# Retention plus two FFN layers on one Trainium2 core: the full-array state products of a chunk moved ahead of its half-width products

## The chip, the cores and the metric

One core of one Trainium2 chip runs the kernel. The metric is device time in microseconds (us) of one execution; kernels are compared by the median of several runs. The engines are named as in the profile: PE (matmuls) with PEld (its weight loads, which have rows of their own), ACT, DVE, POOL, and SP, which issues the DMAs.

## What is computed

Three stages in a row. The first is a retention layer over 2 batches, 8 heads, 768 tokens, head width 64; the other two are feed-forward layers of width 512 to 2048 to 512, the first with Mish, the second with ELU. Cut to its core:

```python
gamma = 1.0 - 2.0 ** (-5.0 - np.arange(H))          # one decay per head
for t in range(S):
    state = gamma * state + k[:, :, t] (outer) v[:, :, t]
    y[:, :, t] = scale * q[:, :, t] @ state
x = y as (B*S, H*D)                                  # 1536 x 512
h = x @ w_in;  x = (h * tanh(softplus(h))) @ w_out   # layer 0
h = x @ w_in2; out = elu(h) @ w_out2                 # layer 1
```

## The kernel before

**Retention.** The recurrence is cut into 12 chunks of 128 tokens, two batches by six positions; chunk `c` belongs to batch `c % 2` and is number `i = c // 2` in its batch. Heads go in four pairs `j`, with `r` = 0, 1 for the head inside a pair. `scores(c)` multiplies keys by queries (16 weight loads, 64 rows each, line 201), and DVE multiplies the result by the decay mask into `at` (line 211). `scale_chunk(c)` lets POOL make `kd` (keys with decay, line 173) and `qd` (queries with decay, line 188). `attend(c)` then builds the output `y`, a 128 x 512 tile of one PSUM bank: for each pair `j` one full-array product of `state[:, j]` with `qd[:, j]` (line 226, 128 rows by 128 columns; left out for `i = 0`), and on top of it two half-width products of `v` with `at` (line 228, 128 rows by 64 columns, one for each half of the partitions). Eight more half-width products make the chunk's own contribution `st` to the state (line 237, left out for the last chunk of each batch). All four kinds are in plain float32, and the trace shows two records ("passes") for each such product.

After the products, `rest()` evacuates: ACT copies `y` to `xh` (line 246), DVE writes the remainder `xl` (line 247) and adds `st` to `state` (line 252, or copies it, line 257, for `i = 0`).

**FFN.** Each FFN layer runs 48 tiles `n`: `up(n)` is 12 full-array matmuls into `h` (line 276, in the order high weights by high x, low weights by high x, high weights by low x), `mish(n)` on ACT and POOL makes `gh` and `gl` (lines 297 to 299), and `down(n - 3)` is 12 full-array matmuls into four accumulators (line 335). Weights arrive packed: SP fetches a half tile (line 101), ACT takes it apart (lines 108, 110), DVE joins it (lines 119, 125), ACT and POOL split it into a high and a low part `w0h`, `w0l` (for `up`) or `w1h`, `w1l` (for `down`) (lines 138, 139). The staging pool has four buffers, so a fetch waits until DVE has joined an earlier half. The first eight tiles of a group each need a new weight tile; the two blocks of eight tiles behind them use the same weights again.

**Order.** Everything stands in one hand-written order, and each engine runs its own instructions in that order. Chunks 0 to 3 come first. Chunks 4 to 11 are laid between the FFN tiles: `scores(4)` behind `up(0)`, `attend(4)` behind `up(1)`, and so on up to `attend(11)` behind `up(15)`. On ACT and DVE the evacuation of a chunk stands in line with the decoding of weights.

Of the kernel before, what the change touches and what calls it, by code (L numbers as in the profile page):

```python
# [21 lines left out]
NPAIR = H // 2  # L22
# [18 lines left out]
def retention_then_two_ffn(  # L41
# [7 lines left out]
    nc = tc.nc  # L49
# [141 lines left out]
    def psum(tag, name):  # L191
        return (psh if tag == "h" else psa).tile([P, NPAIR, P], F32, tag=tag, name=name)
# [23 lines left out]
    def attend(c, tags=("h", "h")):  # L216

        kv = raw.pop(c)[1]
        at, (qd, kd) = scored.pop(c), scaled.pop(c)
        i = c // B  # L220
        v = kv[:, 1]
        state = states[c % B]
        y = psum(tags[0], "y")
        for j in range(NPAIR):
            if i:
                nc.tensor.matmul(y[:, j], state[:, j], qd[:, j], start=True, stop=False)  # L226
            for r in range(2):
                nc.tensor.matmul(  # L228
                    y[r * D:(r + 1) * D, j], v[:, 2 * j + r], at[:, r, j],
                    start=not i, stop=True,  # L230
                )
        if i < CPB - 1:
            st = psum(tags[1], "st")
            for j in range(NPAIR):
                for r in range(2):
                    sl = slice(r * D, (r + 1) * D)
                    nc.tensor.matmul(  # L237
                        st[sl, j, sl], kd[:, 2 * j + r], v[:, 2 * j + r], start=True, stop=True
                    )

        def rest():
            b, o = divmod(c, CPT)
            if o == 0:
                x[b] = new_x(b)
            xh, xl = (a[:, :, o * P:(o + 1) * P] for a in x[b])
            nc.scalar.copy(out=xh, in_=y)  # L246
            nc.vector.tensor_tensor(out=xl, in0=y, in1=xh.bitcast(F32), op=ALU.subtract)
            if i < CPB - 1:
                for r in range(2):
                    sl = slice(r * D, (r + 1) * D)  # L250
                    if i:
                        nc.vector.tensor_tensor(
                            out=state[sl, :, sl], in0=st[sl, :, sl], in1=state[sl, :, sl],
                            op=ALU.add,
                        )
                    else:
                        nc.vector.tensor_copy(state[sl, :, sl], st[sl, :, sl])

        return rest

    def new_x(b):
        return tuple(
            xpool.tile([P, KT, TB], F32R, tag=f"x{n}{b}", name=f"x{n}{b}") for n in "hl"
        )
# [100 lines left out]
    with tc.manual_schedule():  # L365
# [54 lines left out]
        scores(1, th)()  # L420
        scale_chunk(2)
        attend(0, tb)()
        scores(2, ta)()
        load_chunk(4)
        scale_chunk(3)
        scores(3, th)()
        join()
        attend(1, th)()
        split_w()
        attend(2, tb)()  # L430
        join()
        attend(3, ta)()
# [116 lines left out]
```

## Time and profile before

| | us |
|---|---|
| median of 3 runs | 594.63 |
| lowest, highest | 593.89, 594.97 |
| the profiled execution's own time | 593.98 |
| its span (first to last instruction) | 592.2 |
| PE busy in the span | 581.0 |
| PEld busy | 472.2 |
| DVE, ACT, POOL busy | 290.7, 275.1, 270.5 |
| granted TensorE clock | full speed throughout (1.0) |

A busy time is the union of an engine's records. The records of matmuls overlap one another, so that a busy PE may still be losing time between them: for PE one reads the distances of the starts beside the busy time.

### The profile page before, as it was taken

What the parts mean: (1) busy time and instruction counts of PE and PEld (TensorE: products, weight loads), DVE (VectorE), ACT (ScalarE), POOL (GpSimd) and SP (SyncE); (2) the same over time, 40 slices, a digit from 0 to 9 for tenths busy, and PEclk for the clock granted to TensorE, in tenths of its full rate; (3) what the DMA queues carried; (4) which work ended last, traced back from release to release, by engine and by line L of the source; (5) the groups of instructions that cost most, each with busy time, mean ns of one, the idle gap of its engine ahead of it and who ended that gap; (6) DMA issues with size and microseconds to landing.
All of it is one profiled execution on the core that took longest, in us unless ns stands there. A gap on an engine that the chain in (4) does not pass through costs nothing.

```text
span 592.2 us, 7565 instructions
## 1 busy us (share of the span) xinstructions
PE 581.0 (98%) x2934; PEld 472.2 (80%) x2934; DVE 290.7 (49%) x354; ACT 275.1 (46%) x482; POOL 270.5 (46%) x200
## 2 busy tenths in 40 slices
PE   6999999999999999999999999999999999999997
PEld 4677777777888888888888888888888888888885
DVE  3787852113234343100483897433797783434534
ACT  1566532312654654222566485533865853333231
POOL 1688764221454554452395487222366552221221
PEclk9999999999999999999999999999999999999999
DMA  8775543200332332000152133000332100100101
GB/s 320 304 249 209 199 162 113 67 0 12 131 107 76 103 106 97 11 1 0 37 177 80 64 107 106 1 1 1 107 107 86 57 1 0 73 0 2 71 2 71
DMA packets 14724, 50.59 MB, mean 85 GB/s; under 512 B 1632, under 2 KB 1632, under 8 KB 14688
## 3 DMA queue, kind: packets, MB, share of 16 engines
q1 hardware_dynamic: 14688, 50.10, 24.3%
q8 instruction: 23, 0.38, 0.2%
q14 instruction: 13, 0.11, 0.1%
HBM read 46.95 MB, written 3.15 MB: 85 GB/s over the span
## 4 chain that ended last, share of the span: by engine, by line
PE 89%; POOL 4%; DMA 3%; DVE 1%; issue 1%; ACT 0%; SPq 0%; POOLq 0%; DVEq 0%; ACTq 0%
PE a L335 43%; PE h L276 42%; DMA xl<-qkv 2%; PE y L228 1%; PE y L226 1%; POOL w0l L139 1%; DMA kv<-qkv 1%; PE sc L201 1%; POOL gl L299 1%; POOL kd L173 1%; POOL qd L188 1%; DMA st<-w 1%; POOL tab L181 0%; DVE acc L348 0%; PE st L237 0%
## 5 line engine op out<-in xcount | busy, mean ns | idle before, releaser
L299 POOL TENSOR_TENSOR gl<-m,gh 128x512 fp32r<-128x512 f32 x48 | 64.2, 1338 | 137.0 <-ACT m L298 117.0
L289 POOL TENSOR_TENSOR gl<-m,gh 128x512 fp32r<-128x512 f32 x48 | 69.5, 1448 | 106.1 <-ACT gh L288 106.1
L119 DVE SCALAR_TENSOR_TENSOR st<-st 128x512 int32<-128x512 int32 x64 | 72.4, 1139 | 90.2 <-ACT st L110 90.0
L276 PE MATMUL h<-xh,w0l 128*128 128x512 f32 x384 | 102.8, 389 | 1.4 <-POOL w0l L139 1.4
L276 PE MATMUL h<-xh,w0h 128*128 128x512 f32 x384 | 103.1, 390 | 0.2 <-ACT xh L246 0.2
L276 PE MATMUL h<-xl,w0h 128*128 128x512 f32 x384 | 102.7, 389 | 0.0
L297 ACT ACTIVATE gh<-h 128x512 fp32r<-128x512 f32 x48 | 28.6, 597 | 135.1 <-PE h L276 135.0
L307 ACT ACTIVATE e<-c 128x512 f32<-128x512 f32 x48 | 30.4, 632 | 123.4 <-DVE c L306 123.3
L276 PEld LDWEIGHTS h<-xh,w0l 128*128 128x128 f32 x384 | 72.0, 188 | 16.7 <-POOL w0l L139 1.8
L306 DVE TENSOR_SCALAR c<-h 128x512 f32<-128x512 f32 x48 | 33.1, 690 | 106.3 <-PE h L276 106.3
L276 PEld LDWEIGHTS h<-xl,w0h 128*128 128x128 f32 x384 | 72.1, 188 | 15.0
L276 PEld LDWEIGHTS h<-xh,w0h 128*128 128x128 f32 x384 | 71.8, 188 | 15.4 <-ACT xh L246 0.4
L125 DVE SCALAR_TENSOR_TENSOR f<-f,st 128x512 int32<-128x512 int32 x64 | 74.6, 1175 | 3.7
L335 PE MATMUL a<-gh,w1h 128*128 128x512 f32 x192 | 76.2, 397 | 0.0
L335 PE MATMUL a<-gh,w1l 128*128 128x512 f32 x192 | 74.8, 390 | 0.0
L335 PE MATMUL a<-gl,w1h 128*128 128x512 f32 x192 | 74.8, 390 | 0.0
L335 PE MATMUL a<-w1h,gh 128*128 128x512 f32 x192 | 74.7, 389 | 0.0
L335 PE MATMUL a<-w1l,gh 128*128 128x512 f32 x192 | 74.7, 389 | 0.0
L335 PE MATMUL a<-w1h,gl 128*128 128x512 f32 x192 | 74.7, 389 | 0.0
L139 POOL TENSOR_TENSOR w0l<-f,w0h 128x512 fp32r<-128x512 f32 x32 | 43.6, 1365 | 32.4 <-ACT w0h L138 27.8
L139 POOL TENSOR_TENSOR w1l<-f,w1h 128x512 fp32r<-128x512 f32 x32 | 45.7, 1427 | 23.3 <-ACT w1h L138 12.3
L108 ACT ACTIVATE f<-st 128x512 f32<-128x512 f32 x64 | 43.0, 672 | 12.8 <-DMA st<-w 7.5
(65 smaller groups left out, 691.9 us busy)
## 6 DMA issues: line engine op xcount, KB each, us to landing
st<-w SPq DMA_DIRECT2D x64, 512.0 KB, 3.6
qk<-qkv SPq DMA_DIRECT2D x10, 512.0 KB, 5.2
kv<-qkv SPq DMA_DIRECT2D x10, 512.0 KB, 5.9
out<-acc SPq DMA_DIRECT2D x12, 256.0 KB, 2.1
xh<-qkv SPq DMA_DIRECT2D x2, 512.0 KB, 9.5
xl<-qkv SPq DMA_DIRECT2D x2, 512.0 KB, 9.7
ct<-consts SPq DMA_DIRECT2D x1, 512.0 KB, 5.4
ct<-consts SPq DMA_DIRECT2D x1, 284.0 KB, 7.2
```

What stands on the lines that cost most here:

```text
L108: nc.scalar.activation(out=f, in_=t[:, :, 1].bitcast(F32), func=AF.Copy, scale=2.0 ** -112)
L119: nc.vector.scalar_tensor_tensor(out=t[:, :, 1], in0=t[:, :, 1], scalar=-(2 ** 31), in1=t[:, :, 0], op0=ALU.bitwise_and, op1=ALU.bitwise_or,)
L125: nc.vector.scalar_tensor_tensor(out=f, in0=f, scalar=3, in1=t[:, :, 1], op0=ALU.logical_shift_left, op1=ALU.bitwise_or,)
L139: nc.gpsimd.tensor_tensor(out=lo, in0=f, in1=hi.bitcast(F32), op=ALU.subtract)
L173: nc.gpsimd.tensor_tensor(out=kd, in0=kv[:, 0], in1=tk[:, i].to_broadcast([P, H, D]), op=ALU.mult)
L276: nc.tensor.matmul(h, u[:, k * P:(k + 1) * P], v[:, k], start=i == 0, stop=i == len(passes) - 1)
L289: nc.gpsimd.tensor_tensor(out=gl, in0=g, in1=gh.bitcast(F32), op=ALU.subtract)
L297: nc.scalar.activation(out=gh, in_=h, func=AF.Mish)
L299: nc.gpsimd.tensor_tensor(out=gl, in0=g, in1=gh.bitcast(F32), op=ALU.subtract)
L306: nc.vector.tensor_scalar(out=c, in0=h, scalar1=0.0, scalar2=None, op0=ALU.min)
L307: nc.scalar.activation(out=e, in_=c, func=AF.Exp)
L335: nc.tensor.matmul(a, l, r, start=first and i == 0, stop=last and i == 2)
```

## The change

In `attend`, the loop over the pairs is split in two. First the four state products of the chunk run one behind the other; then the eight half-width products. Before, each pair's state product stood ahead of its two half-width products, and each state product had `start=True`, which begins a new sum; now only the first of them has it (one clearing of the bank for the whole chunk), and the other three carry no start flag. Chunks with `i = 0` have no state products, and their eight half-width products keep their flags. `skip_group_check=True` only tells the builder not to check the grouping of the sums.

```diff
         y = psum(tags[0], "y")
+        if i:
+            for j in range(NPAIR):
+                nc.tensor.matmul(
+                    y[:, j], state[:, j], qd[:, j],
+                    start=j == 0, stop=False, skip_group_check=True,
+                )
         for j in range(NPAIR):
-            if i:
-                nc.tensor.matmul(y[:, j], state[:, j], qd[:, j], start=True, stop=False)
             for r in range(2):
                 nc.tensor.matmul(
                     y[r * D:(r + 1) * D, j], v[:, 2 * j + r], at[:, r, j],
-                    start=not i, stop=True,
+                    start=not i, stop=True, skip_group_check=True,
                 )
```

What stands on PE for chunk 6, between `up(5)` and `down(2)`, before (`state_98` is the state of batch 0; a row is a run of equal products, the last number its count; in brackets, whose semaphores it waits for):

```order
L276 MATMUL h<-xl_188,w0h 128x512 x4
L226 MATMUL y<-qd,state_98 128x128
L228 MATMUL y<-at,kv 64x128 [waits DMAHW7_49,DVE_49]
L228 MATMUL y<-at,kv 64x128 [waits DVE_49]
L226 MATMUL y<-qd,state_98 128x128
L228 MATMUL y<-at,kv 64x128 x2
L226 MATMUL y<-qd,state_98 128x128
L228 MATMUL y<-at,kv 64x128 x2
L226 MATMUL y<-qd,state_98 128x128
L228 MATMUL y<-at,kv 64x128 x2
L237 MATMUL st<-kv,kd 64x64 [waits PE_49]
```

and at the same place after:

```order
L282 MATMUL h<-xl_188,w0h 128x512 x4
L228 MATMUL y<-qd,state_98 128x128 x4
L234 MATMUL y<-at,kv 64x128 [waits DMAHW7_49,DVE_49]
L234 MATMUL y<-at,kv 64x128 [waits DVE_49]
L234 MATMUL y<-at,kv 64x128 x6
L243 MATMUL st<-kv,kd 64x64 [waits PE_49]
```

The products and the waits are the same; three state products have moved ahead of the first half-width product. (Lines from 226 on have new numbers.)

Chunk 3, the last one ahead of `up(0)`, on PE, before (`state_99` is the state of batch 1, `xl_224` and `xl_117` hold this chunk's `at` and `v`):

```order
L226 MATMUL y<-qd,state_99 128x128 [waits DVE_49,PE_49,Pool_49]
L228 MATMUL y<-xl_224,xl_117 64x128 [waits DMAHW2_49]
L228 MATMUL y<-xl_224,xl_117 64x128
L226 MATMUL y<-qd,state_99 128x128
L228 MATMUL y<-xl_224,xl_117 64x128 x2
L226 MATMUL y<-qd,state_99 128x128
L228 MATMUL y<-xl_224,xl_117 64x128 x2
L226 MATMUL y<-qd,state_99 128x128
L228 MATMUL y<-xl_224,xl_117 64x128 x2
L237 MATMUL st<-xl_117,kd 64x64 [waits PE_49]
L237 MATMUL st<-xl_117,kd 64x64 x7
L276 MATMUL h<-xh_187,w0h 128x512 [waits Activation_49]
```

and after:

```order
L228 MATMUL y<-qd,state_99 128x128 [waits DVE_49,PE_49,Pool_49]
L228 MATMUL y<-qd,state_99 128x128 x3
L234 MATMUL y<-xl_224,xl_117 64x128 [waits DMAHW2_49]
L234 MATMUL y<-xl_224,xl_117 64x128 x7
L243 MATMUL st<-xl_117,kd 64x64 [waits PE_49]
L243 MATMUL st<-xl_117,kd 64x64 x7
L282 MATMUL h<-xh_187,w0h 128x512 [waits Activation_49]
```

Here too only the three later state products have moved; the chunk's first product still waits for DVE and POOL, and `up(0)` for ACT. No other engine's order changes.

## Rows read from the trace of the kernel before

**Rows 1.** The page: busy time by engine (part 1), chain that ended last (part 4).

```profile
PE 581.0 (98%) x2934; PEld 472.2 (80%) x2934; DVE 290.7 (49%) x354; ACT 275.1 (46%) x482; POOL 270.5 (46%) x200
...
PE 89%; POOL 4%; DMA 3%; DVE 1%; issue 1%; ACT 0%; SPq 0%; POOLq 0%; DVEq 0%; ACTq 0%
```

**Rows 2.** What PE waited for: us in total, times, longest.

```profile
PE h L276 <- POOL w0l L139: 1.4, 1, 1.4
PE y L226 <- POOL qd L188: 1.0, 1, 1.0
```

**Rows 3.** Timeline of PE, chunk 6: start, us, line, shapes, passes.

```profile
60.20 0.38 PE L226 MATMUL y<-qd,state 128*128 128x128 f32 x2
60.52 0.44 PE L228 MATMUL y<-at,kv 128*64 128x128 f32 x4
60.88 0.49 PE L226 MATMUL y<-qd,state 128*128 128x128 f32 x2
61.30 0.44 PE L228 MATMUL y<-at,kv 128*64 128x128 f32 x4
...
63.15 0.63 PE L237 MATMUL st<-kv,kd 128*64 128x64 f32 x16
```

**Rows 4.** What PEld waited for, same columns as rows 2.

```profile
PEld y L226 <- issue: 5.4, 31, 0.2
```

**Rows 5.** Chain of waits in order of time, chunk 6: start, length, what.

```profile
60.37 0.22 PE y L226 x2
60.59 0.37 PE y L228 x4
60.96 0.42 PE y L226 x2
```

**Rows 6.** Timeline of PE, chunk 1, which has no state products.

```profile
15.13 1.09 PE L228 MATMUL y<-xl,kv 128*64 128x128 f32 x16
16.05 0.64 PE L237 MATMUL st<-kv,kd 128*64 128x64 f32 x16
```

**Rows 7.** Groups by line and shape, PE: count, busy us, mean ns, idle before.

```profile
L226 PE MATMUL y<-qd,state 128*128 128x128 f32 x80 | 18.7, 315 | 1.1 <-POOL qd L188 1.0
```

**Rows 8.** Timeline of PE, first 62 us: chunks 2 and 3, up(0), up(5).

```profile
17.67 0.49 PE L226 MATMUL y<-qd,state 128*128 128x128 f32 x2 [0.99 <-POOL qd L188]
...
21.48 0.46 PE L226 MATMUL y<-qd,state 128*128 128x128 f32 x2
...
25.36 1.20 PE L276 MATMUL h<-xh,w0h 128*128 128x512 f32 x4 [0.22 <-ACT xh L246]
...
58.25 1.19 PE L276 MATMUL h<-xh,w0l 128*128 128x512 f32 x4 [1.38 <-POOL w0l L139]
```

**Rows 9.** Timeline of DVE: state copy of chunk 1, xl of chunk 4.

```profile
20.49 0.84 DVE L257 COPY state<-st 64x256 f32<-64x256 f32 x2
...
36.11 0.69 DVE L247 TENSOR_TENSOR xl<-y,xh 128x512 fp32r<-128x512 f32 x1 [2.38 <-POOL gl L299]
```

**Rows 10.** Timeline of ACT: copies of y for chunks 3 and 4, a later decode.

```profile
24.72 0.58 ACT L246 CAST xh<-y 128x512 fp32r<-128x512 f32 x1 [2.05 <-PE y L228]
...
35.43 0.58 ACT L246 CAST xh<-y 128x512 fp32r<-128x512 f32 x1 [1.05 <-PE y L228]
...
44.58 0.69 ACT L108 ACTIVATE f<-st 128x512 f32<-128x512 f32 x1 [2.20 <-DMA st<-w]
```

**Rows 11.** Timeline of POOL: gl of tile 3, low weights of tiles 5 and 7.

```profile
46.87 1.29 POOL L299 TENSOR_TENSOR gl<-m,gh 128x512 fp32r<-128x512 f32 x1 [3.88 <-ACT m L298]
...
56.93 1.26 POOL L139 TENSOR_TENSOR w0l<-f,w0h 128x512 fp32r<-128x512 f32 x1
...
71.96 1.29 POOL L139 TENSOR_TENSOR w0l<-f,w0h 128x512 fp32r<-128x512 f32 x1
```

**Rows 12.** Timeline of PE: up(7), second group of four, which reads w0l.

```profile
74.23 1.07 PE L276 MATMUL h<-xh,w0l 128*128 128x512 f32 x4
```

**Rows 13.** Stretch 60 to 145 us: length, busy us (records) by engine, clock, DMA.

```profile
60.00:145.00 85.00, 85.00 (x543) 66.17 (x542) 29.26 (x38) 28.18 (x51) 36.35 (x28) 1.00 0.28 94
```

## The prediction

> **What bounds the kernel now.** Read the busy times first: PE is at 98% and every other engine below half of the span [rows 1]; the chain that ended last is PE for 89% [rows 1]. Then where PE stands still: after the first loads it waits 1.0 us for `qd` at chunk 2 and 1.4 us for `w0l` at `up(5)`, and hardly elsewhere [rows 2]. From 60 us to 145 us, where chunks 6 to 11 lie, PE is busy 85.00 of 85.00 us, at a granted clock of 1.00 (the 2.4 GHz level), while ACT, DVE and POOL work 28 to 36 us [rows 13]. So from `up(5)` on, whatever shortens PE's stream shortens the run; ahead of it the question is which waits take the gain.
>
> Busy does not mean full. In chunk 6 [rows 3] the second pair's state product starts at 60.88 and its half-width products at 61.30, 0.42 later; the first pair's two half-width products took from 60.52 to 60.88, 0.36. A pair thus costs 0.42 + 0.36 = 0.78 us. The weight loads show the gap: ahead of the state products PEld idles 31 times, 5.4 us in all, 0.17 each, with nothing that it waits for by name [rows 4]. 31 is three times for each of the ten chunks with a state product, and one: each return from half-width to full-array work. The chain says the same in another way [rows 5]: two state passes cost 0.22 behind full-array work and 0.42 behind half-width work.
>
> **The change, part by part.** The products are the same, with the same shapes and waits. Moved are three state products in each of ten chunks (2 to 11), and with them three turns to half-width and three turns back go away.
>
> *A chunk today*: first state product at 60.20, first `st` product at 63.15: 2.95 us [rows 3].
>
> *A chunk after*: four state products, then eight half-width ones.
> - Three state products followed by another state product: 0.22 each, as the chain has it behind full-array work [rows 5]: 0.66. No row shows two different state products in a row. Lower bound 0.22 less a rounding; upper bound 0.42, a product whose weights are loaded with nothing beside them [rows 5]. I take 0.22, since PEld is busy 66.17 us beside a PE that is busy all 85.00 [rows 13]: loads run beside full-array matmuls.
> - The last state product and the turn: first state pass to first half-width pass, 60.20 to 60.52 [rows 3]: 0.32.
> - Eight half-width products in a row, opening included: 15.13 to 16.05 in chunk 1, which has no state products [rows 6]: 0.92.
>
> Sum 0.66 + 0.32 + 0.92 = 1.90, so a chunk is 1.05 us shorter; with the start-to-start distances unrounded it is nearer 1.07. I use 1.06. The single clearing of the bank changes a flag, no instruction: nothing, bounded by 0.05 a chunk either way from the spread of these rows.
>
> The Trainium skill's page "TensorE: Matmul & The Clock Gate", section "Back-to-back issue gap", gives a sustained 81 ns for each matmul of 128 columns in a stream with weight loads. By that estimate a state product is 0.16, a chunk 0.18 shorter still, and eight chunks end at 584.7; the trace's 0.11 a pass [rows 5] decides.
>
> *Which of the ten count.*
> - Chunk 2 starts at 17.67, when `qd` comes [rows 8]; its 1.06 us go. Chunk 3 starts at 21.48 [rows 8], behind DVE's copy of its state, which ends at 20.49 + 0.84 = 21.33 [rows 9] and hangs on the decoding of the first weights, not on chunk 2. Worth 0.
> - Chunk 3 ends earlier by 1.06. ACT's copy at 24.72 waited for it [rows 10], and `up(0)` at 25.36 waited for ACT [rows 8]. Worth 1.06.
> - Chunk 4: the same, for `up(2)`. And its end releases ACT's copy at 35.43 [rows 10], from which the decoding goes on: DVE's `xl` at 36.11 [rows 9], its state addition and joins, the next fetch, whose data ACT awaits for 2.20 at 44.58 [rows 10], `gl` on POOL at 46.87, and POOL's unbroken queue up to `w0l` of tile 5 at 56.93 [rows 11], for which PE waits until 58.25 [rows 8]. With both chunks this queue moves by 2.12. Worth 1.06.
> - Chunk 5 ends earlier still, but nothing in that queue waits for its end: `w0l` comes at the time just given. PE's wait at `up(5)`, with some of it at `up(4)`, grows from 1.4 to about 2.5. Worth 0.
> - Chunks 6 to 11: PE never stands still there [rows 13]; 6 x 1.06 = 6.36. The nearest supply is `w0l` of tile 7: ready at 71.96 + 1.29 = 73.25 [rows 11], read at 74.23 [rows 12], 0.98 to spare; ACT and POOL make it right behind `up(6)`, so it moves with PE. After tile 7 weights are used again, and POOL is free more than half of the time [rows 13].
>
> Total 1.06 + 1.06 + 6.36 = 8.5 us. The profiled execution took 593.98 us, 592.2 of it span, which gives 585.5; the median of the runs shown is 0.65 above it, and from there 594.63 - 8.5 = 586.1. That is the forecast; its own range is 585.3 to 586.9 (0.05 on each of eight chunks, and half a microsecond in the supply queue).
>
> **The rivals.**
>
> *A. The supply queue before 60 us does not follow chunk 4.* The trace names POOL's `gl` as what DVE's `xl` at 36.11 waited for [rows 9], not ACT's copy, which ended at 35.43 + 0.58 = 36.01. If so, the queue follows only chunk 3, by up to 1.06, or nothing: 6.36 to 7.42 us, 587.2 to 588.3. Against it: of POOL's results `xl` can only need the reading of the `xl1` buffer by `qd` of chunk 3, long done by then, and 36.01 and 36.11 fit ACT.
>
> *B. Full-array products do not overlap.* Loading the next state weights might wait for the matmul before. Then three products cost 0.42 each, 0.60 more a chunk; 0.46 is saved, times eight 3.7 us: 590.9. The Trainium skill's page "TensorE: Matmul & The Clock Gate", Part 3, "The mechanism", speaks for it: a weight load runs beside matmuls in flight only if it goes to another row group. State products all use the same rows, and so do the FFN's, in which the 66.17 us of loads beside an unbroken PE [rows 13] disagree with it.
>
> *C. Slower.* A state product might hold the array for the whole duration of its two records, 2 x 0.315 = 0.63 us [rows 7], before the next one starts, because all four add up in one bank. The chunk is then 3 x 0.63 + 0.32 + 0.92 = 3.13, 0.18 longer, and eight give 596.1. It turns from gain to loss at (2.95 - 1.24) / 3 = 0.57 a product. Against it: today two passes of the same product, into the same bank, follow 0.11 apart [rows 5].
>
> *D. More.* If chunks 2 and 5 count too (another order of the early waits) or the passes come closer: up to 10 x 1.06 = 10.6, 584.0.
>
> *E. Nothing.* The turns might cost the same in any order, or PE's queue regroup products already today; 594.6. Against it: rows 3 and 4 show a gap at every turn, in the written order.
>
> **How the numbers follow.** Forecast 0.72, A 0.11, B 0.05, C 0.03, D 0.06, E 0.03. The range reaches down to D's upper half, 584.3, and up to the end of A, 588.4; outside lie B, C, E and a part of D, some 0.14. Within 0.2% (1.2 us, about what a measurement of this kernel can tell from no change) is E; slower is C; faster the rest, 0.94.
>
> **What would show it.** In the profile after: a chunk from its first state pass to its first `st` pass in about 1.89 us; the idle times of PEld ahead of state products down from 31 to at most a few; state passes merged in runs of eight; PE's wait for `w0l` at `up(5)` at 2 to 2.5 us and that matmul at about 56.1 instead of 58.25; chunk 11 some 7.4 us earlier at its start, 8.5 at its end, and everything behind it too. B shows as state products 0.42 apart; C as 0.63 apart; A as `up(5)`'s low products only 0 to 1.06 earlier. The forecast is wrong if a new wait stands in chunks 6 to 11, for `at`, `qd` or weights.

## The result and the profile after

The changed kernel takes 586.63 us (median, 586.22 to 587.09), the kernel before in the same comparison 594.68 us (593.89 to 594.97). The ratio is 0.9867, with a 95% interval of 0.985 to 0.9884: 8.05 us less. The forecast was 586.1 us, 8.5 us less. The profiled execution of the changed kernel took 586.22 us, 584.4 of it span; that of before took 593.98 us, so the two traces that are compared here differ by 7.8 us. The granted clock is 1.00 in both (the 2.4 GHz level).

Line numbers from 226 on have moved: the state product is now L228, the half-width product L234, `st` L243, `up`'s products L282, the first of the products behind the chunks L341.

The page, the two lines that answer to [rows 1]:

```profile
PE 571.4 (98%) x2934; PEld 470.5 (81%) x2934; DVE 292.0 (50%) x354; ACT 275.4 (47%) x482; POOL 272.1 (47%) x200
...
PE 93%; DMA 3%; POOL 2%; DVE 1%; ACT 0%; issue 0%; SPq 0%; POOLq 0%
```

PE has the same 2934 records and is busy 9.6 us less. PEld's busy time is about the same (470.5 against 472.2), as it should be if no load is saved and only the gaps between loads go.

The timeline of PE at chunk 6 (start, us, line, shapes, passes), which answers to [rows 3]:

```profile
58.37 1.05 PE L228 MATMUL y<-qd,state 128*128 128x128 f32 x8
59.36 1.09 PE L234 MATMUL y<-at,kv 128*64 128x128 f32 x16
60.28 0.64 PE L243 MATMUL st<-kv,kd 128*64 128x64 f32 x16
```

From the first state pass to the first `st` pass it is 60.28 - 58.37 = 1.91 us, where it was 2.95. The chain of waits has the state products as eight passes in 0.89 us, 0.11 each, which answers to [rows 5]:

```profile
58.54 0.89 PE y L228 x8
```

What PE waited for, in us, times, longest, which answers to [rows 2]:

```profile
PE h L282 <- POOL w0l L139: 2.2, 2, 1.7
...
PE y L228 <- DVE state L263: 1.2, 1, 1.2
```

The wait for `w0l` has grown from 1.4 to 2.2 us and a wait of chunk 3 for DVE's copy of the state has come up; the 1.0 us for `qd` is as before. In PEld's list the row of [rows 4], 31 idle times with nothing waited for by name, is gone; its largest is now

```profile
PEld h L282 <- POOL w0l L139: 3.4, 3, 2.1
```

Before it was one wait of 1.8 us. Of the two that are new one is at `up(4)`, the other at `up(7)`; the latter is where the change lost something behind 60 us, and it is taken up below.

### The profile page after: what moved, and what is told of

The parts are those of the page before. It is cut to its first block, busy times and chain, and to the rows that moved or that the text cites. A ratio compares the mean times of both kernels' runs of the same rounds, so it can differ in the third digit from the quotient of the medians.

```text
span 584.4 us, 7565 instructions
## 1 busy us (share of the span) xinstructions
PE 571.4 (98%) x2934; PEld 470.5 (81%) x2934; DVE 292.0 (50%) x354; ACT 275.4 (47%) x482; POOL 272.1 (47%) x200
## 4 chain that ended last, share of the span: by engine, by line
PE 93%; DMA 3%; POOL 2%; DVE 1%; ACT 0%; issue 0%; SPq 0%; POOLq 0%
PE a L341 44%; PE h L282 44%; DMA st<-w 2%; PE y L234 2%; PE y L228 1%; PE sc L201 1%; DMA ct<-consts 1%; PE st L243 0%; DVE acc L354 0%; POOL w0l L139 0%; POOL qd L188 0%; POOL kd L173 0%; POOL tab L181 0%; DVE f L125 0%; POOL gl L305 0%; POOL w1l L139 0%
## 5 line engine op out<-in xcount | busy, mean ns | idle before, releaser
L119 DVE SCALAR_TENSOR_TENSOR st<-st 128x512 int32<-128x512 int32 x64 | 73.9, 1161 | 90.3 <-ACT st L110 90.2
L282 PE MATMUL h<-xh,w0l 128*128 128x512 f32 x384 | 103.1, 390 | 2.2 <-POOL w0l L139 2.2
L282 PE MATMUL h<-xh,w0h 128*128 128x512 f32 x384 | 103.1, 390 | 0.2 <-ACT xh L252 0.2
L282 PE MATMUL h<-xl,w0h 128*128 128x512 f32 x384 | 102.7, 389 | 0.0
L282 PEld LDWEIGHTS h<-xh,w0l 128*128 128x128 f32 x384 | 71.9, 188 | 18.3 <-POOL w0l L139 3.4
L282 PEld LDWEIGHTS h<-xl,w0h 128*128 128x128 f32 x384 | 72.1, 188 | 15.0
L282 PEld LDWEIGHTS h<-xh,w0h 128*128 128x128 f32 x384 | 71.7, 188 | 15.3 <-ACT xh L252 0.4
L341 PE MATMUL a<-gh,w1h 128*128 128x512 f32 x192 | 76.2, 397 | 0.0
L341 PE MATMUL a<-gl,w1h 128*128 128x512 f32 x192 | 74.9, 390 | 0.0
L341 PE MATMUL a<-gh,w1l 128*128 128x512 f32 x192 | 74.8, 389 | 0.0
L341 PE MATMUL a<-w1h,gh 128*128 128x512 f32 x192 | 74.7, 389 | 0.0
L341 PE MATMUL a<-w1l,gh 128*128 128x512 f32 x192 | 74.7, 389 | 0.0
L341 PE MATMUL a<-w1h,gl 128*128 128x512 f32 x192 | 74.7, 389 | 0.0
```

The lines of the kernel that those rows point to most:

```text
L119: nc.vector.scalar_tensor_tensor(out=t[:, :, 1], in0=t[:, :, 1], scalar=-(2 ** 31), in1=t[:, :, 0], op0=ALU.bitwise_and, op1=ALU.bitwise_or,)
L282: nc.tensor.matmul(h, u[:, k * P:(k + 1) * P], v[:, k], start=i == 0, stop=i == len(passes) - 1)
L341: nc.tensor.matmul(a, l, r, start=first and i == 0, stop=last and i == 2)
```

## The experiments

Four theories say why the chunk got shorter, and two questions are about where its gain went.

- Theory 1, the prediction's: each turn from full-array to half-width products and back costs PE about 0.35 us, and the change takes three of four away.
- Theory 2: the four clearings of the bank cost, and the change leaves one.
- Theory 3: the gain needs all four state products in one unbroken run; the number of turns does not count.
- Theory 4: what costs is that sums of two kinds take turns in the bank, not the products' width.
- Where the gain went: do chunks 2 and 5 count, and what limits the early stretch?

All experiments but the one at full width keep every product of the kernel; they change the order of the products, one flag, or the place of one POOL instruction. Those on the grouping replace the two loops by

```
groups = [[j] for j in range(NPAIR)]          # the order of before
for g in groups:
    if i:
        for j in g:
            nc.tensor.matmul(
                y[:, j], state[:, j], qd[:, j],
                start=j == 0, stop=False, skip_group_check=True,
            )
    for j in g:
        for r in range(2):
            nc.tensor.matmul(
                y[r * D:(r + 1) * D, j], v[:, 2 * j + r], at[:, r, j],
                start=not i, stop=True, skip_group_check=True,
            )
```

and differ in `groups` alone. In their traces the state product is L230, the half-width product L236, `st` L245 and `up` L284.

### One clearing, the order of before

`groups` as printed.

> The order of before (one state product, two half-width products, pair by pair), but one clearing of the bank per chunk, as in the change. Theory 1, the turns between full-array and half-width work cost the time: nothing changes, 594.7 us, a chunk from its first state pass to its first st pass 2.95 us. Theory 2, the clearings cost it (each start flag holds the array until the bank is quiet): 586.6 us like the changed kernel, chunk 1.91.

Measured: 594.10 us (593.75 to 594.56) against 594.03 for before, ratio 1.000 (0.999 to 1.0009). PE's timeline at chunk 6, in the first rows and the first row of `st`:

```profile
60.31 0.38 PE L230 MATMUL y<-qd,state 128*128 128x128 f32 x2
60.63 0.44 PE L236 MATMUL y<-at,kv 128*64 128x128 f32 x4
...
63.26 0.64 PE L245 MATMUL st<-kv,kd 128*64 128x64 f32 x16
```

63.26 - 60.31 = 2.95 us, to the hundredth that of before, and PEld's idle times are back:

```profile
PEld y L230 <- issue: 5.4, 31, 0.2
```

So the number of clearings costs and gains nothing that shows, which is what the prediction had put it at. Theory 2 falls.

### Two and two

```diff
-groups = [[j] for j in range(NPAIR)]
+groups = [(0, 1), (2, 3)]
```

> Two state products, their four half-width products, and the same again: one turn and return taken out of three stays, two go. One clearing per chunk. Theory 1: each turn and return costs a third of the 1.04 us that a chunk gained, so a chunk takes 2.95 - 0.69 = 2.26 us and the run some two thirds of the gain, 594.7 - 5.4 = 589.3 us. Theory 2 (clearings): 586.6. Theory 3, the gain needs the unbroken run of state products: 594.7.

Measured: 589.08 us, ratio 0.9926 (0.99 to 0.9953). PE's timeline at chunk 6, whole:

```profile
59.23 0.61 PE L230 MATMUL y<-qd,state 128*128 128x128 f32 x4
59.77 0.66 PE L236 MATMUL y<-at,kv 128*64 128x128 f32 x8
60.35 0.71 PE L230 MATMUL y<-qd,state 128*128 128x128 f32 x4
60.99 0.66 PE L236 MATMUL y<-at,kv 128*64 128x128 f32 x8
61.48 0.63 PE L245 MATMUL st<-kv,kd 128*64 128x64 f32 x16
```

61.48 - 59.23 = 2.25 us: two turns fewer than before save 0.70, three save 1.04, so 0.35 each. PEld's idle times follow the count, ten where it was 31 and none in the change, one for each chunk:

```profile
PEld y L230 <- issue: 1.7, 10, 0.2
```

The price goes by the number of turns. Theory 3 falls.

### Full width in the order of before

```diff
-        y[r * D:(r + 1) * D, j], v[:, 2 * j + r], at[:, r, j],
-        start=not i, stop=True, skip_group_check=True,
+        y[:, j], v[:, 2 * j:2 * j + 2].rearrange("p h d -> p (h d)"), at[:, r, j],
+        start=not i and r == 0, stop=r == 1,
```

The order is that of before, with a state product and then two of the others for each pair, but all of them now use the whole array. The output then holds cross terms between the two heads of a pair, so this run is good for times only.

> The order of before, pair by pair, but each half-width product of v with at replaced by a full-array one with the two heads' v side by side (128 columns), so that the output holds cross terms between the heads. Theory 1, the turns between widths cost the time: ahead of the state products PEld no longer idles, every product takes 0.22 us, a chunk 12 x 0.22 + 0.1 to 0.2 for the one turn to st, some 2.8 us, although it does more work than the chunk of the changed kernel (1.91). Rival, it is the alternation between two kinds of sums in one bank that costs: gaps of 0.17 us stay ahead of the state products, and a chunk takes 3.2 us or more.

Measured once: 593.71 us, beside 594.16 for before. PE's timeline at chunk 6 (the lines are those of before):

```profile
61.34 0.38 PE L226 MATMUL y<-qd,state 128*128 128x128 f32 x2
61.55 0.61 PE L228 MATMUL y<-at,kv 128*128 128x128 f32 x4
62.00 0.39 PE L226 MATMUL y<-qd,state 128*128 128x128 f32 x2
...
64.11 0.57 PE L237 MATMUL st<-kv,kd 128*64 128x64 f32 x12
```

64.11 - 61.34 = 2.77 us. The eight products are now full-array work and one pair takes 62.00 - 61.34 = 0.66 us, less than the 0.78 of before, though its two half products ran side by side. PEld has one idle time left ahead of state products, and it is another thing, 1.4 us at once, at the start of chunk 3:

```profile
PEld y L226 <- issue: 1.4, 1, 1.4
```

State and other products still take turns in the bank; only the width no longer changes, and the gap is gone. Theory 4 falls, and theory 1 stands: the change of width is what costs. The Trainium skill's page "TensorEngine Tiling (Array Packing)", section "Key Properties", says that changing the tiling mode, unlike going to another tile, drains the array; it gives no duration. The rows above agree with it, and put 0.35 us on a turn with its return here. Whether the array drains at a turn, or the next weights merely cannot be loaded ahead of it, no run here tells apart.

### Chunks 2 and 5 alone

```diff
-groups = [[j] for j in range(NPAIR)]
+groups = [range(NPAIR)] if c in (2, 5) else [[j] for j in range(NPAIR)]
```

> The changed order in chunks 2 and 5 alone, the order of before in the other eight. If chunk 2 is swallowed by the wait for the state copy and chunk 5 by the wait for low weights at up(5): no gain, 594.7 us within 0.4, both chunks 1.04 shorter, PE's wait for w0l about 1.0 longer than the 1.4 of before. Rival, each chunk counts: 2.1 less, 592.6.

Measured: 594.20 us (594.00 to 594.68), ratio 1.0003 (0.9994 to 1.0013). PE's timeline, chunk 5 and then the low-weight products of `up(4)` and `up(5)`:

```profile
42.59 1.05 PE L230 MATMUL y<-qd,state 128*128 128x128 f32 x8
...
44.49 0.64 PE L245 MATMUL st<-kv,kd 128*64 128x64 f32 x16
...
49.73 1.19 PE L284 MATMUL h<-xh,w0l 128*128 128x512 f32 x4 [0.73 <-POOL w0l L139]
...
58.50 1.20 PE L284 MATMUL h<-xh,w0l 128*128 128x512 f32 x4 [1.71 <-POOL w0l L139]
```

Chunk 5 does get shorter, 1.90 us, and PE gives the whole of it back: it waits 0.73 + 1.71 = 2.4 us for `w0l` where it waited 1.4 [rows 2], and `up(5)` reads `w0l` at 58.50, no earlier than the 58.25 of before [rows 8]. Worth nothing that shows, as the prediction had it.

### All but chunks 2 and 5

```diff
-groups = [[j] for j in range(NPAIR)]
+groups = [range(NPAIR)] if c not in (2, 5) else [[j] for j in range(NPAIR)]
```

> The changed order in all chunks but 2 and 5. If those two are worth nothing: the whole gain, 586.6 us within 0.4, and PE's wait for w0l at up(5) about 1 us shorter than in the changed kernel. Rival, each chunk counts: 588.7.

Measured: 587.22 us (586.61 to 588.56), ratio 0.9885 (0.9863 to 0.9906). The median lies 0.6 us above the value expected, with an interval that overlaps with that of the change. In its profiled execution `up(5)` reads `w0l` at 57.50, a good microsecond behind the change's 56.42, and PE's wait there is 1.69 us, about as long as the change's 1.72 and not 1 us shorter as expected: the weights came later too. The chain of waits names one fetch of weights:

```profile
38.69 5.06 DMA st<-w
```

It was issued at the same moment as in the change (38.67), and ACT waited for it until 43.84, where it decodes at 42.75 in the change. The landing took 5.06 us here, 4.0 in the trace of the change and 3.85 in that of before. To tell one late landing from chunks 2 and 5, it was run again, beside the change itself:

> The changed kernel itself, beside the next two on one chip. 8.05 us below the kernel before, as measured (0.9867 with an interval of 0.985 to 0.9884).

> The changed order in all chunks but 2 and 5, again, now on the same chip as the changed kernel. Chunks 2 and 5 worth nothing: the two times agree within 0.5 us; the distance of some 1 us seen between the single profiles is then the landing of one fetch (4.0 us after its issue at 38.67 in the changed kernel, 5.1 us after 38.69 here). Rival, the two chunks are worth something: 0.6 to 2.1 us slower than the changed kernel.

Measured on the one chip: the change 586.85 us, ratio 0.9879 (0.9864 to 0.9894), and without chunks 2 and 5 586.90 us, 0.9881 (0.9864 to 0.9897). They are 0.05 us apart; the rival's 2.1 us is excluded, a few tenths are not, since the single runs of the second kernel lie between 586.46 and 587.72. So chunks 2 and 5 are worth nothing that shows.

The late landing, however, was not one execution's. The chain of waits has it again in both traces, first in that of the change:

```profile
38.16 4.94 DMA st<-w
```

and in that without chunks 2 and 5:

```profile
38.74 5.06 DMA st<-w
```

`up(5)` reads `w0l` at 56.81 and 57.50 there, and PE's waits for `w0l` come to 2.6 and 2.3 us. It is the first trace of the change, with 4.0 us, that stands at the short end: over all traces this fetch took 3.9 to 4.3 us in the four in which chunks 3 and 4 have the order of before or full width (it is issued at 40.5 to 41.5 there), and 4.0 to 5.1 us in the eight in which these chunks are shorter and it is issued at 38.2 to 38.9. Why it takes longer there stays open.

### Can the wait for low weights be had too?

Two edits aim at the 2.2 us that PE now waits for POOL's `w0l`. The first makes the table of chunk 6 (`tab`, on POOL) at tile 2 instead of tile 3 (at 42.28 in its trace, at 50.27 in the change's), in a second buffer, so that it no longer stands right ahead of the `w0l` of tile 5:

```diff
-tabs[i] = qd_p.tile([P, NPAIR, P], F32, tag="tab", name="tab")
+tabs[i] = qd_p.tile([P, NPAIR, P], F32, tag="tab", name="tab", bufs=2)
...
+            if n == 2:
+                make_tab(3)
```

> The changed kernel, with one POOL instruction moved: the table for chunk 6 (1.49 us) is made two tiles earlier, in POOL's idle time before gl of tile 3, into a second buffer. If POOL's queue ahead of the low weights of tile 5 is what holds PE at up(5) and takes chunk 5's gain: PE's wait for w0l there falls from 1.7 to about 0.2 us and the time by some 1.3 us against the changed kernel, to 585.3 where that shows 586.6. Rival, the queue follows the arrival of the data (the fetch) and not POOL's work: no change, the wait stays at 1.7.

Measured: 586.17 us (585.11 to 587.45), ratio 0.9868 (0.9852 to 0.9884). PE's timeline at the low-weight products of `up(5)` and `up(7)`:

```profile
55.42 1.20 PE L284 MATMUL h<-xh,w0l 128*128 128x512 f32 x4 [0.76 <-POOL w0l L139]
...
71.24 1.20 PE L284 MATMUL h<-xh,w0l 128*128 128x512 f32 x4 [0.65 <-POOL w0l L139]
```

The wait at `up(5)` fell from 1.72 to 0.76 us, not to the expected 0.2. Beside the change run again on the same chip, `up(5)` comes 1.39 us earlier (56.81 there), but at `up(7)` (71.93 there) 0.69 is left: the weights of tile 7 are the next limit. The expected 585.3 us was not reached, and the interval overlaps with the change's.

The second edit lets `up` read the low weights in its last group of products instead of the second:

```diff
-for u, v in ((hi, xh), (lo, xh), (hi, xl))
+for u, v in ((hi, xh), (hi, xl), (lo, xh))
```

> The changed kernel, with the second and third group of up() exchanged: high weights by high x, high weights by low x, low weights by high x. The low weights are then wanted one group (0.92 us) later. If what is left of the loss sits in the supply of low weights at up(4), up(5) and up(7): PE's waits there shrink from 0.5, 1.7 and 0.2 us to 0, 0.8 and 0, and the time by about 0.9 us, to 585.9 where the changed kernel shows 586.8. Rival, the supply follows PE (each earlier product only moves the wait to the next tile): within 0.3 of the changed kernel.

Measured: 585.97 us (585.59 to 586.03), ratio 0.9865 (0.9849 to 0.9882). One wait for `w0l` is left, at `up(5)`:

```profile
57.37 1.19 PE L282 MATMUL h<-xh,w0l 128*128 128x512 f32 x4 [1.31 <-POOL w0l L139]
```

It is 1.31 us and not the expected 0.8, and by its ratio this kernel is not clear of the change (0.9867, and 0.9879 when run again).

Both together:

> The same, with the table for chunk 6 made early as in the run before. That run gained 1.0 us at up(5) and gave most of it back at up(7), where PE waited 0.65 us for low weights. With 0.92 us more room at both: 0.9 below that run, about 585.3, and no wait at up(7). Rival: no better than the exchange alone.

Measured: 585.53 us (584.51 to 586.20), ratio 0.9858 (0.9844 to 0.9873). PE waits no more for `w0l`, and 0.6 us for ACT's high weights instead:

```profile
PE h L284 <- ACT w0h L138: 0.6, 1, 0.6
```

This is the lowest median of all, but its interval overlaps with that of the change run again (0.9864 to 0.9894), so that it beats the change is not shown.

## Why the prediction was right, step by step

**The chunk.** Predicted 1.90 us, measured 1.91. Its parts fit too: first state pass to first half-width pass 59.36 - 58.37 = 0.99 (three times 0.22 and 0.32 make 0.98), half-width products 60.28 - 59.36 = 0.92, as in chunk 1 [rows 6]. So what no row of before showed, different state products in a row, runs at the price that two passes behind full-array work had [rows 5]. Rival B falls, and with it its mechanism: state products on the same rows of the array follow each other 0.11 us a pass, while the loads go on beside them. The Trainium skill's page "TensorE: Matmul & The Clock Gate", Part 3, "The mechanism", has a line by which a load runs beside matmuls in flight only when it goes to another row group; these rows disagree with that line, and the measurement decides. They would fit another sentence of the same section, by which a load that goes to the background weight buffer is pulled ahead as well. Rival C falls at the same row: a state product takes 0.22 us, not 0.63.

What a chunk saves was put at 1.06; it is 2.95 - 1.91 = 1.04. Over eight chunks that is 0.16 us of the forecast's excess.

**Chunks 2 and 5: nothing.** Right to within a few tenths, by two experiments (594.20 beside 594.03 us with them alone; 586.90 beside 586.85 us without them). PE's timeline of the change shows where chunk 2's gain goes:

```profile
17.81 1.16 PE L228 MATMUL y<-qd,state 128*128 128x128 f32 x8 [0.99 <-POOL qd L188]
...
21.61 1.13 PE L228 MATMUL y<-qd,state 128*128 128x128 f32 x8 [1.16 <-DVE state L263]
...
24.45 1.20 PE L282 MATMUL h<-xh,w0h 128*128 128x512 f32 x4 [0.22 <-ACT xh L252]
```

Chunk 3 starts at 21.61, 0.13 later than before [rows 8], because DVE's copy is no earlier; the new wait of 1.16 us is chunk 2's gain. The start-up of this execution is 0.14 us behind that of before (17.81 against 17.67), and `up(0)` is 0.91 earlier, 1.04 less that.

**Chunks 3 and 4: 2.12 predicted, 1.83 measured.** `up(5)`'s low products start at

```profile
56.42 1.19 PE L282 MATMUL h<-xh,w0l 128*128 128x512 f32 x4 [1.72 <-POOL w0l L139]
```

and not at 56.1. The queue does follow both chunks: ACT's copy for chunk 4 went from 35.43 to

```profile
33.51 0.58 ACT L252 CAST xh<-y 128x512 fp32r<-128x512 f32 x1
...
42.75 0.69 ACT L108 ACTIVATE f<-st 128x512 f32<-128x512 f32 x1 [2.36 <-POOL w1l L139]
```

1.92 earlier, two chunks of 1.04 less 0.13 of start-up (1.95), and the decode from 44.58 [rows 10] to 42.75, which is the 1.83 of `up(5)`. So of the 0.29 that are missing, 0.04 is the size of a chunk, some 0.13 the start-up and the rest, 0.1, the fetch and the decode in between. These tenths are one execution's: in the change run again, where the fetch took 4.94 us, `up(5)` reads at 56.81, only 1.44 earlier than before. The prediction moved this fetch along with its issue, at an unchanged length. PE's waits at `up(4)` and `up(5)` came to 2.2 us, predicted 2 to 2.5.

Rival A falls by that: the queue moved by more than its 1.06. The row that spoke for it is there again. It is DVE's `xl` of chunk 4, for which the profile names POOL's `gl`:

```profile
34.17 0.69 DVE L253 TENSOR_TENSOR xl<-y,xh 128x512 fp32r<-128x512 f32 x1 [1.23 <-POOL gl L305]
```

POOL makes two `gl` one behind the other there. In the change the first ends at 32.36 + 1.73 = 34.09,

```profile
32.36 1.73 POOL L305 TENSOR_TENSOR gl<-m,gh 128x512 fp32r<-128x512 f32 x1
```

and the two together end at 32.36 + 2.99 = 35.35, when `xl` has been running for 1.2 us. In the trace of before the first ended at 33.13 + 1.73 = 34.86, and the second, at 34.82 + 1.27 = 36.09,

```profile
34.82 1.27 POOL L299 TENSOR_TENSOR gl<-m,gh 128x512 fp32r<-128x512 f32 x1
```

just ahead of `xl` at 36.11 [rows 9]. Neither `gl` fits both traces: the first was done 1.25 us too early before, the second comes too late after. ACT's copy fits both: it ended at 36.01 ahead of 36.11, and at 33.51 + 0.58 = 34.09 ahead of 34.17. It was ACT.

**Chunks 6 to 11: 6.36 predicted, 5.9 measured.** PE is busy 85.00 of 85.00 us here as well; the row of the stretch, as [rows 13]:

```profile
60.00:145.00 85.00, 85.00 (x561) 69.90 (x556) 31.04 (x40) 29.38 (x54) 38.53 (x29) 1.00 0.33 106
```

The last of the chunks and what follows, and the row that follows it in the trace of before:

```profile
132.29 1.05 PE L228 MATMUL y<-qd,state 128*128 128x128 f32 x8
...
134.29 0.50 PE L341 MATMUL a<-gh,w1h 128*128 128x512 f32 x1
```

```profile
142.04 0.50 PE L335 MATMUL a<-gh,w1h 128*128 128x512 f32 x1
```

Chunk 11 starts at 132.29 and started at 139.00, 6.71 us earlier (predicted 7.4). It ends at 134.29 and ended at 142.04, so 7.75 us are saved by then (predicted 8.5), and the traces' spans differ by 7.8. Less the 1.83 of `up(5)`, chunks 6 to 11 gave 5.92: six times 1.04 is 6.24, and 0.3 is lost on the way.

**The step that failed** is small, and it is the sentence that `w0l` of tile 7 "moves with PE" and has 0.98 to spare. By the prediction's own sign, a new wait for weights in chunks 6 to 11, it was wrong there. PE comes to `up(7)` earlier by 1.83 and by chunk 6's 1.04, in all 2.87. POOL's `w0l` was ready at 73.25 [rows 11]; now it is ready at 69.66 + 1.75 = 71.41, only 1.84 earlier. 2.87 - 1.84 = 1.03, and the 0.98 are gone. PE's timeline at `up(7)`, the second row of which answers to [rows 12]:

```profile
70.48 1.07 PE L282 MATMUL h<-xh,w0h 128*128 128x512 f32 x4
71.46 1.21 PE L282 MATMUL h<-xh,w0l 128*128 128x512 f32 x4
72.51 1.09 PE L282 MATMUL h<-xl,w0h 128*128 128x512 f32 x4
```

From start to start that is 0.98 and 1.05 us, where a group of four takes 0.91 unhindered, as they do at `up(8)`: 0.2 us lost, while PEld waited 0.33 for `w0l`. The change run again shows the same (1.04 and 1.03 us).

What `w0l` moved with instead is POOL's own queue. In the trace of before POOL stood idle for 0.96 us ahead of `gl` of tile 6, which hangs on PE's `up(6)`, and `w0l` of tile 7 followed that `gl`:

```profile
70.65 1.35 POOL L299 TENSOR_TENSOR gl<-m,gh 128x512 fp32r<-128x512 f32 x1 [0.96 <-ACT m L298]
```

That much was right. In the change POOL has no such gap; from `gl` of tile 5 to `w0l` of tile 7 it works without a break:

```profile
61.06 1.30 POOL L305 TENSOR_TENSOR gl<-m,gh 128x512 fp32r<-128x512 f32 x1 [2.99 <-ACT m L304]
...
66.28 1.71 POOL L188 TENSOR_TENSOR qd<-qk,tab 128x512 f32<-128x512 f32 x1
67.96 1.74 POOL L305 TENSOR_TENSOR gl<-m,gh 128x512 fp32r<-128x512 f32 x1
69.66 1.75 POOL L139 TENSOR_TENSOR w0l<-f,w0h 128x512 fp32r<-128x512 f32 x1
```

This `gl` of tile 5 started at 62.75 before, so the queue moved by 1.69, as far as ACT's decode that stands ahead of it (60.45 to 58.74, both behind a fetch), and not by PE's 2.87. POOL used up its 0.96 of idle time, but `gl` of tile 6 and `w0l` took 0.39 and 0.46 longer than before: 1.69 + 0.96 - 0.85 = 1.80, the 1.84 but for rounding.

Beside these two stand DVE's joins of tile 7's words, which got longer as well; DVE's timeline of the change:

```profile
66.79 3.46 DVE L125 SCALAR_TENSOR_TENSOR f<-f,st 128x512 int32<-128x512 int32 x2
```

In the trace of before the same two took 2.37 us, with POOL idle for 0.96 of them:

```profile
68.46 2.37 DVE L125 SCALAR_TENSOR_TENSOR f<-f,st 128x512 int32<-128x512 int32 x2
```

The joins did not hold `w0l` up themselves: ACT's `w0h`, made from the first of them, was done at 68.58 + 0.62 = 69.20, and `w0l` starts where POOL's `gl` ends.

The last 0.1 us of the loss is spread over chunks 7 to 11 (4.09 earlier by four chunks, 1.02 each) and has no wait that the profile names. The chunk itself saves its 1.04 there too; the products of `down` right behind it take 0.02 longer (behind chunk 8, for one, 90.74 to 93.61 where it was 95.41 to 98.26).

**The sum**: 0.16 for the size of a chunk, 0.25 in the early queue and 0.3 behind it are 0.7 less than 8.5, which gives the 7.8 that the traces differ by. Rival D's extra gain isn't there, and E falls. The gain itself is known less well than these tenths suggest. In the second comparison the change took 586.85 us and the kernel before 594.16, 7.3 us more; in the three later comparisons the kernel before lies at 593.9 to 594.2 and not at 594.7. So the forecast gain was too large by 0.5 to 1.2 us, and that the forecast time came within 0.6 us of the measured one is in part the luck of a high starting value.

## What to carry to other kernels

Where products that fill the array alternate with products that use half of its columns, count the turns: grouping them by width took 0.35 us off PE for each turn and return here, at no cost, and idle times of the weight loads with nothing named as waited for were the mark of it. Before multiplying a gain by the number of places, ask at each what the next late thing hangs on: two of ten chunks gave all of it back to a wait, and at `up(7)` the time to spare was gone because the supply's queue had moved with an earlier chunk than its reader. The name that a profile gives as releaser can be tested with a second trace: a true releaser ends just ahead of its reader in both.

## What the runs showed of the hardware

- More array work was shorter: with full-array products in place of half-width ones, in the alternating order, a chunk took 2.77 us instead of 2.95. In a run of their own, half-width passes come 0.92 / 16 = 0.058 us apart, full-array passes 0.89 / 8 = 0.11.
- DVE's joins take 1.73 us each (3.46 / 2) when POOL works beside both, 1.19 on the mean (2.37 / 2) when it is idle for part of them, and 0.64 (1.28 / 2) in the row below, while POOL is idle from 58.08 to 61.06. POOL's `w0l` grows from 1.29 [rows 11] to 1.75. The Trainium skill's page "SBUF — State Buffer", section "Who interferes with whom", names these two engines as the only ones that contend there, one blocking the other for a whole instruction; the rows agree with contention, and which of the two waited for the other in each place is not shown.

```profile
58.54 1.28 DVE L125 SCALAR_TENSOR_TENSOR f<-f,st 128x512 int32<-128x512 int32 x2
```

- The same fetch, issued at 38.67 in the trace of the change and at 38.69 in the first one without chunks 2 and 5, took 4.0 and 5.06 us; its reader started 1.1 us apart (42.75 and 43.84), and `up(5)` read its low weights as much apart. Over twelve traces the fetch took 3.9 to 5.1 us. Differences of a microsecond in the early stretch are not to be read from one trace.
